# RWKV-6 attention with a mixture-of-depths block: reordering GpSimd's and ScalarE's turn, the loads, the PSUM pair and the steps table

## The chip, the cores and the metric

The kernel runs on one core of a Trainium2 chip. The metric is the device time of one execution in microseconds (us); runs of one kernel are compared by their medians.

## What is computed

The first part is a recurrence over 768 positions for 4 batches of 8 heads of 48 dimensions. The second part takes the 384 numbers of a position (8 heads side by side) as one row, scores the 768 rows of a batch, picks the 128 best of them, sends these through a small two-layer network and adds the gated outcome to them.

```python
for t in range(S):
    cur = einsum('bhd,bhe->bhde', u * k[t], v[t])
    y[t] = einsum('bhd,bhde->bhe', r[t], state + cur)
    state = w[t][..., None] * state + einsum('bhd,bhe->bhde', k[t], v[t])
...
scores = einsum('bsd,d->bs', x, w_gate)
for b in range(B):
    top_idx = argpartition(-scores[b], 128)[:128]
    xe = x[b, top_idx]
    ye = maximum(xe @ w1, 0) @ w2            # 384 -> 1024 -> 384
    g = sigmoid(scores[b, top_idx])
    out[b, top_idx] = xe + g[:, None] * ye
```

## The kernel before

The positions of a batch are cut into 6 chunks of 128, which gives 24 chunks, numbered n from 0 to 23. The recurrence is done chunk by chunk with matrix products. Within a chunk the products of the decays are taken from the start of the chunk, so that k is multiplied by a falling factor and r by a rising one; scores inside the chunk, the contribution of the state before the chunk, and the new state are then products of these.

The program order of every engine's queue is the order in which the code issues the instructions; no scheduler changes it. One pass of the loop in the last part of the kernel is called turn n here. A turn works on several chunks at once, each at another stage:

- `loads(n + 4)` (L102) issues on SP's queue the loads of w for chunk n+8, of k and r for chunk n+7 and of v for chunk n+5. In seven early turns a piece of the network's weights follows (L545).
- `from_state(n)` (L301) multiplies r of chunk n by the state on TensorE (PE); a small copy `seen` (L309) on ScalarE (ACT) follows it.
- `lnw(n + 4)` takes on ACT the logarithm lw of w (L139) and, from it, `over` (L143).
- `divided(n + 3)` (L183) makes kw on GpSimd (POOL).
- `scores(n + 1)` (L242), `fresh(n + 1)` (L258) and `from_chunk(n)` (L318) are three more sets of 32 small matmuls on PE.
- `turned(n + 2, ...)` (L226, L228) transposes K and R on PE into a pair of PSUM tiles (`psR`, tag "r") and copies them out on ACT as Kt and Rt.
- `masked`, `states` and `result` (L270, L285, L288, L332, L338) run on VectorE (DVE): the masked scores sc, the states s1 and mid, the output x of chunk n and its score. `states` ends with the product s on POOL (L290), which needs a small row `all_buf`. `result` sends x to memory on SP's queue (L342) and needs `vo`.
- `sums(n + 4)` adds lw up on PE (L159) into a PSUM tile of the pool `psM` (tag "m", one buffer); ACT makes `fall` and `rise` (L162, L165) and, on one partition, `line_buf` (L172), and SP's queue spreads this to `all_buf` (L176).
- `scaled(n + 3)` (L216) makes K and R on DVE.
- `own_products(n + 3)` (L192, L193) makes rk on POOL in two products, the first of which waits for `scaled`; `own_values(n + 1)` (L207) makes `vo` on POOL; `own_sum(n + 2)` (L200) is on DVE.

The second part of a batch runs in the turns of the next batch, in small steps. `select(b)` is a generator with these steps: spread the scores (ps_e and `every`, twice), count for each position how many are ahead of it (`ahead`, six pieces, L369), the `rank` (ps_r, L379) and the pick matrix (`pick`, L393), then the row numbers (ps_i, L400, `idx`) and the gather of the rows (`xe`, L413, an indirect transfer from POOL's queue), the transpose of these (ps_x, L421, `xeT`), and the gate. Its PSUM tiles share the one buffer "m" with `sums`. `forward(b)` has 16 steps: eight of three products with w1 (L464), with an activation `hid` (L469) after the fourth and the eighth, and eight of one product with w2 (L474), the last of which also makes `ye` (L480) and scatters it (L483). Its PSUM tile is a single buffer "f". In the profile every such product is two matmuls.

The table `plan` says which steps a turn takes: for each sixth of a batch two strings, the first run behind `from_chunk`, the second at the end of the turn; "s" is a step of `select`, "f" one of `forward`. `forward(b)` joins the queue of steps in the turn that `plan_forward` names.

After the loop, for the last batch, the kernel first decides whether all decays were in range: a sum of `guard` on DVE (L574), a matmul (L576), a comparison `wide` (L578), and a load of it into a register on all engines (L581). Then the rest of the second part follows, in an order written out as one string. A general version for decays out of range stands behind a branch and is not taken.

Of the kernel before, what the change touches and what calls it, by code (L numbers as in the profile page):

```python
# [9 lines left out]
FP32 = mybir.dt.float32  # L10
# [3 lines left out]
AF = mybir.ActivationFunctionType  # L14
# [3 lines left out]
L = 128  # L18
# [17 lines left out]
def kernel(  # L36
# [59 lines left out]
    def load(name, n):  # L96
        if not 0 <= n < N:
            return
        b, ci = chunks[n]
        x, bufs = dict(w=(w, 5), k=(k, 5), r=(r, 5), v=(v, 6))[name]  # L100
        t = lev.tile([L, H, D], FP32, tag=name, name=name, bufs=bufs)
        nc.sync.dma_start(  # L102
            out=t, in_=x[b, :, ci * L:(ci + 1) * L, :].rearrange("h t d -> t h d")
        )
        work[n][name] = t

    def loads(n):
        load("w", n + 4)
        load("k", n + 3)
        load("r", n + 3)  # L110
        load("v", n + 1)

    weights = [
        (w1[:, c], moe_w1[c * L:(c + 1) * L, :]) for c in range(NDC)
# [38 lines left out]
    def sums(n):  # L153
        if not 0 <= n < N:
            return
        t = work[n]
        lw = t.pop("lw")
        ps = psM.tile([L, 512], FP32, tag="m", name="ps_x")
        nc.tensor.matmul(ps[:, 0:C], tri, lw, start=True, stop=True)  # L159
        t["fall"] = lev.tile([L, C], FP32, tag="fall", name="fall")  # L160
        t["rise"] = lev.tile([L, C], FP32, tag="rise", name="rise")
        nc.scalar.activation(  # L162
            out=t["fall"], in_=ps[:, 0:C], func=AF.Exp, accum_out=guard[:, n, 1:2]
        )
        nc.scalar.activation(  # L165
            out=t["rise"], in_=ps[:, 0:C], func=AF.Exp, scale=-1.0,
            accum_out=guard[:, n, 0:1],
        )
        if chunks[n][1] > 0:
            line = line_bufs[n % len(line_bufs)]  # L170
            t["all"] = all_bufs[n % len(all_bufs)]
            nc.scalar.activation(  # L172
                out=line[:, :, 0:D, :].rearrange("o q d j -> o j q d"), func=AF.Exp,
                in_=ps[0:1, 0:C].rearrange("o (j q d) -> o j q d", q=2, d=D),
            )
            nc.sync.dma_start(out=t["all"], in_=line.rearrange("o q d j -> o (q d j)"))  # L176

# [171 lines left out]
    def select(b):  # L349

        every = mod.tile([L, S], FP32, name="every")
        for hf in range(2):
            ps = psM.tile([L, NHF, L], FP32, tag="m", name="ps_e")
            for q in range(NHF):
                c = hf * NHF + q
                nc.tensor.transpose(
                    ps[:, q, :], score[:, b, c:c + 1].to_broadcast([L, L]), ident
                )
            nc.scalar.copy(  # L359
                out=every[:, hf * NHF * L:(hf + 1) * NHF * L],  # L360
                in_=ps.rearrange("p q t -> p (q t)"),
            )
            yield

        ahead = mod.tile([L, NCH, S], BF16, name="ahead")
        won = mod.tile([L, NCH], FP32, name="won", bufs=2)
        for c in range(NCH):
            lo = c * L
            nc.vector.scalar_tensor_tensor(  # L369
                out=ahead[:, c, lo:S], in0=every[:, lo:S], scalar=score[:, b, c:c + 1],  # L370
                in1=behind[:, 0:S - lo], op0=ALU.is_le, op1=ALU.mult,
                accum_out=won[:, c:c + 1],
            )
            if c != NCH - 2:
                yield
        ps = psM.tile([L, NCH], FP32, tag="m", name="ps_r")
        for c in range(NCH):
            for e in range(c + 1):
                nc.tensor.matmul(  # L379
                    ps[:, c:c + 1], ahead[:, e, c * L:(c + 1) * L], ones[:, 0:1],  # L380
                    start=(e == 0), stop=(e == c),
                )
        rank = mod.tile([L, NCH], FP32, name="rank", bufs=2)
        nc.vector.tensor_sub(rank, behind_n, won)
        nc.vector.tensor_add(rank, ps, rank)

        for gi, (c0, n) in enumerate(groups):
            pick = mod.tile([L, NCH, L], BF16, name="pick")
            at = rank
            if c0 > 0:  # L390
                at = mod.tile([L, NCH], FP32, name="at")
                nc.vector.tensor_scalar_add(out=at, in0=rank, scalar1=float(-c0))
            nc.vector.tensor_tensor(  # L393
                out=pick, in0=_heads(slots, NCH), in1=at.to_broadcast([L, NCH, L]),
                op=ALU.is_equal,
            )
            yield
            ps = psM.tile([L, 2], FP32, tag="m", name="ps_i")
            for c in range(NCH):
                nc.tensor.matmul(  # L400
                    ps, pick[:, c, :], ids[:, b, c, :], start=(c == 0), stop=(c == NCH - 1)
                )
            idx = mod.tile([L, 1], UINT32, name="idx", bufs=2)
            nc.vector.tensor_scalar(
                out=idx, in0=ps[:, 0:1], scalar1=ps[:, 1:2], scalar2=float(b * S),
                op0=ALU.add, op1=ALU.max,
            )
            rows = views[b][0:b + 1].rearrange("b s c -> (b s) c")
            where = bass.IndirectOffsetOnAxis(ap=idx[0:n, 0:1], axis=0)
            xe = mod.tile([L, C], FP32, name="xe", bufs=2)  # L410
            if n < L:
                nc.vector.memset(xe, 0.0)
            nc.gpsimd.indirect_dma_start(  # L413
                out=xe[0:n], out_offset=None, in_=rows, in_offset=where,
                bounds_check=(b + 1) * S - 1, oob_is_err=False,
            )
            yield

            ps = psM.tile([L, NDC, L], FP32, tag="m", name="ps_x")
            for dc in range(NDC):  # L420
                nc.tensor.transpose(ps[:, dc, :], xe[:, dc * L:(dc + 1) * L], ident)  # L421
            xeT = mod.tile([L, NDC, L], FP32, name="xeT", bufs=2)
            nc.scalar.copy(out=xeT, in_=ps)
            yield

            own = mod.tile([L, 1], FP32, name="own", bufs=2)
            scr = lev.tile([L, C], FP32, tag="scr", name="scr")
            nc.vector.tensor_tensor_reduce(
                out=scr, in0=xe, in1=wg_bc, scale=1.0, scalar=0.0, op0=ALU.mult, op1=ALU.add,
                accum_out=own,  # L430
            )
            neg = mod.tile([L, 1], FP32, name="neg", bufs=2)
            nc.vector.scalar_tensor_tensor(
                out=neg, in0=own, scalar=-1.0, in1=own, op0=ALU.mult, op1=ALU.min
            )
            nc.scalar.activation(out=neg, in_=neg, func=AF.Exp)
            den = mod.tile([L, 1], FP32, name="den", bufs=2)
            nc.vector.tensor_scalar_add(out=den, in0=neg, scalar1=1.0)
            nc.vector.reciprocal(out=den, in_=den)
            gate = mod.tile([L, 1], FP32, name="gate", bufs=2)  # L440
            nc.vector.scalar_tensor_tensor(
                out=gate, in0=own, scalar=0.0, in1=neg, op0=ALU.is_ge, op1=ALU.max
            )
            nc.vector.tensor_mul(gate, gate, den)
            chosen.setdefault(b, []).append((n, rows, where, xe, xeT, gate))
            yield
            if len(groups) > 1:
                yield from forward(b)
# [40 lines left out]
    def run(*steps):  # L489
        for g in steps:  # L490
            yield from g

    plan = [
        ("", "fsfsss"), ("", "fssfsf"), ("", "fsf"), ("s", "fff"), ("s", "sfff"), ("", "fff")
    ]
    plan_forward = 4 * NCH // 6
    steps = dict(s=iter(()), f=iter(()))

    def mix(what):

        for x in what:
            next(steps[x], None)
# [3 lines left out]
    with tc.manual_schedule():  # L506
# [34 lines left out]
        for n in range(-4, N):  # L541
# [10 lines left out]
                if j == plan_forward:  # L552
                    steps["f"] = run(steps["f"], forward(b))
            from_state(n)
            lnw(n + 4)
            divided(n + 3)
            scores(n + 1)
            fresh(n + 1)
# [1 line left out]
            mix(what[0])  # L560
            turned(n + 2, "K")
            turned(n + 2, "R")
            masked(n + 1)
            states(n + 1)
            result(n)
            sums(n + 4)
            scaled(n + 3)
            own_products(n + 3)
            own_values(n + 1)
            own_sum(n + 2)  # L570
            mix(what[1])

        total = setup.tile([L, 1], FP32)
        nc.vector.tensor_reduce(out=total, in_=guard, axis=AX.XY, op=ALU.add)  # L574
        ps = psM.tile([L, C], FP32, tag="m", name="ps_w")
# [3 lines left out]
            out=wide, in0=ps[0:1, 0:1], scalar1=LIMIT, scalar2=0.5, op0=ALU.is_le, op1=ALU.is_lt  # L579
        )  # L580
        wide = nc.values_load(wide, min_val=0, max_val=1)  # L581

        steps["s"] = run(steps["s"], select(B - 1))
        mix("ssssfsfsfsfsfsffff" + "s")
        mix(1000 * "f" + 1000 * "s")
        for _ in forward(B - 1, "mr"):
            pass
# [72 lines left out]
```

## Time and profile before

| | us |
|---|---|
| median of 3 runs (221.84 to 223.57) | 223.22 |
| profiled execution, its own time | 223.47 |
| profiled execution, span of the profile | 221.6 |

| engine | busy us | share of the span |
|---|---|---|
| PE | 172.4 | 78% |
| DVE | 141.6 | 64% |
| POOL | 117.6 | 53% |
| ACT | 102.2 | 46% |

The x of chunk 0 starts at 27.87 us, that of chunk 6 at 64.54, of chunk 12 at 107.24, of chunk 18 at 152.55, and that of chunk 23 at 188.67. The rest is the second part of the last batch. In a row of the order of time, the first number is the start, the second the duration in us; a bracket at the end tells how long the engine had been idle and what released it. In a row of the waits, the numbers are the total in us, the times, and the longest.

### The profile page before, as it was taken

Reading aid. Unit: us, or ns where it says so; the run is one execution under the profiler, and the core shown is the slowest. Engines: PE = TensorE matmul, PEld = TensorE weight load, DVE = VectorE, ACT = ScalarE, POOL = GpSimd, SP = SyncE. Lnnn points to the kernel's source line nnn. Section 1 sums busy time; section 2 is a strip of 40 time slices with the busy share of each in tenths; the row PEclk is TensorE's granted clock in tenths of the full one; section 3 lists DMA queues with packets and bytes.
Section 4 is the critical chain, followed back from the end, with each engine's and each line's share of the span. In section 5 each row is a group of like instructions: output and inputs, shape, how many; then the busy total and the mean of one; then the engine's idle time right before and its main releaser. Section 6 shows DMA issues by size and latency. Waiting matters only on the chain.

```text
span 221.6 us, 8505 instructions
## 1 busy us (share of the span) xinstructions
PE 172.4 (78%) x3586; PEld 138.2 (62%) x3586; DVE 141.6 (64%) x329; ACT 102.2 (46%) x261; POOL 117.6 (53%) x137
## 2 busy tenths in 40 slices
PE   2697677797859766897799869978898598686990
PEld 0465466676648665796687657867876467553950
DVE  6443177777546998695769986976499834281301
ACT  4685645476852722755666426656642101110110
POOL 3750578887176669775546497745654931001101
PEclk9998899999985985999999969999999769999997
DMA  6998997878989996996899884622011022101101
GB/s 130 209 186 168 192 176 163 177 137 224 233 199 210 213 209 166 198 230 149 180 201 210 180 179 100 157 63 73 3 40 40 4 70 74 38 1 36 38 7 40
DMA packets 108542, 29.38 MB, mean 133 GB/s; under 512 B 103376, under 2 KB 107728, under 8 KB 108496
## 3 DMA queue, kind: packets, MB, share of 16 engines
q1 hardware_dynamic: 107984, 27.18, 56.5%
q0 software_dynamic: 512, 1.57, 2.1%
q8 instruction: 30, 0.49, 1.0%
q14 instruction: 16, 0.13, 0.2%
HBM read 23.20 MB, written 5.51 MB: 130 GB/s over the span
## 4 chain that ended last, share of the span: by engine, by line
PE 27%; DVE 21%; issue 13%; POOL 11%; DMA 9%; ACT 9%; SPq 8%; POOLq 0%; DVEq 0%; ACTq 0%
SPq L102 6%; DMA all_buf<-line_buf 5%; PE ps_p L318 5%; PE ps_f L464 5%; DVE ahead L369 5%; PE ps_t L226 5%; POOL rk L192 3%; DVE scr L338 3%; POOL vo L207 3%; DVE x L332 3%; PE ps_f L474 3%; POOL rk L193 2%; DVE k_buf L216 2%; DMA xe<-out_dram,idx 2%; PE ps_p L242 2%
## 5 line engine op out<-in xcount | busy, mean ns | idle before, releaser
L192 POOL TENSOR_TENSOR rk<-r,k 128x384 f32<-128x384 f32 x24 | 24.4, 1015 | 20.7 <-DVE r_buf L216 19.4
L228 ACT COPY Kt<-ps_t 128x512 f32<-128x512 f32 x24 | 14.0, 585 | 45.1 <-PE ps_t L226 45.1
L318 PE MATMUL ps_p<-v,sc 64*64 64x48 f32 x768 | 30.8, 230 | 4.4 <-issue 2.6
L290 POOL TENSOR_TENSOR s<-mid,all_buf 128x192 f32<-128x192 f32 x20 | 12.2, 610 | 38.7 <-DMA all_buf<-line_buf 24.1
L318 PEld LDWEIGHTS ps_p<-v,sc 64*64 64x64 f32 x768 | 28.0, 146 | 5.6 <-issue 3.0
L159 PE MATMUL ps_x<-lw,tri 128*128 128x384 f32 x48 | 23.9, 585 | 6.4 <-ACT lw L139 6.4
L369 DVE SCALAR_TENSOR_TENSOR ahead<-every,score,behind 128x768 bf16<-128x768 f32 (+5 forms) x24 | 23.4, 1024 | 8.2 <-ACT every L359 8.2
L464 PE MATMUL ps_f<-xeT,w 128*128 128x128 f32 x192 | 24.5, 278 | 4.5 <-ACT hid L469 3.9
L464 PEld LDWEIGHTS ps_f<-xeT,w 128*128 128x128 f32 x192 | 23.1, 192 | 7.5 <-ACT hid L469 4.5
L193 POOL TENSOR_TENSOR rk<-rk,u_bc 128x384 f32<-128x384 f32 x24 | 25.2, 1050 | 1.9
L183 POOL TENSOR_TENSOR kw<-k,over 128x384 f32<-128x384 f32 x24 | 24.4, 1018 | 3.0 <-DMA k<-in_k_dram 2.9
L474 PE MATMUL ps_f<-w,hid 128*128 128x384 f32 x64 | 25.3, 529 | 0.7 <-ACT hid L469 0.7
L270 DVE TENSOR_TENSOR sc<-ps_p,mask 128x512 f32<-128x512 f32 x24 | 16.4, 682 | 14.7 <-PE ps_p L258 14.7
L332 DVE TENSOR_TENSOR x<-ps_p,vo 128x384 f32<-128x384 f32 x24 | 13.3, 552 | 17.4 <-POOL vo L207 14.5
L207 POOL TENSOR_TENSOR vo<-v,own 128x384 f32<-128x384 f32 x24 | 23.2, 966 | 0.0
L242 PE MATMUL ps_p<-Rt,Kt 48*64 48x64 f32 x768 | 17.7, 229 | 5.6 <-DVE x L332 3.2
L301 PEld LDWEIGHTS ps_p<-s,Rt 48*64 48x64 f32 x704 | 13.5, 135 | 13.4 <-issue 7.3
L242 PEld LDWEIGHTS ps_p<-Rt,Kt 48*64 48x64 f32 x768 | 15.0, 141 | 7.3 <-ACT over L143 2.0
L226 PE MATMUL ps_t<-ident,k_buf 128*128 128x128 f32 x96 | 18.7, 327 | 0.0
L301 PE MATMUL ps_p<-s,Rt 48*64 48x48 f32 x704 | 16.4, 223 | 2.5 <-DVE mid L288 2.5
L474 PEld LDWEIGHTS ps_f<-w,hid 128*128 128x128 f32 x64 | 12.6, 208 | 8.0 <-issue 1.8
L226 PE MATMUL ps_t<-ident,r_buf 128*128 128x128 f32 x96 | 17.2, 310 | 0.0
(77 smaller groups left out, 301.8 us busy)
## 6 DMA issues: line engine op xcount, KB each, us to landing
w<-in_w_dram SPq DMA_DIRECT2D x24, 192.0 KB, 4.0
k<-in_k_dram SPq DMA_DIRECT2D x24, 192.0 KB, 4.4
r<-in_r_dram SPq DMA_DIRECT2D x24, 192.0 KB, 4.7
v<-in_v_dram SPq DMA_DIRECT2D x24, 192.0 KB, 4.0
out_dram<-x SPq DMA_DIRECT2D x24, 192.0 KB, 2.8
w<-in_moe_w_dram SPq DMA_DIRECT2D x3, 512.0 KB, 5.2
w<-in_moe_w_dram SPq DMA_DIRECT2D x4, 384.0 KB, 5.2
all_buf<-line_buf SPq DMA_DIRECT2D x20, 2.0 KB, 2.6
```

What stands on the lines that cost most here:

```text
L159: nc.tensor.matmul(ps[:, 0:C], tri, lw, start=True, stop=True)
L183: nc.gpsimd.tensor_mul(t["kw"], t["k"], t.pop("over").rearrange("p (h d) -> p h d", d=D))
L192: sync(nc.gpsimd.tensor_mul(rk, t.pop("r"), t.pop("k")), t["scaled"], "one port")
L193: nc.gpsimd.tensor_mul(rk, rk, u_bc)
L207: nc.gpsimd.tensor_mul(t["vo"], t["v"], t.pop("own").to_broadcast([L, H, D]))
L226: nc.tensor.transpose(ps[:, j, :], t[name][:, 2 * j:2 * j + 2, :], ident)
L242: nc.tensor.matmul(P[half(sub), par, j * HB:(j + 1) * HB], t["Kt"][half(par, D), j, half(sub)], t["Rt"][half(par, D), j, half(sub)], start ...
L301: nc.tensor.matmul(t["P"][half(sub), par, j * D:(j + 1) * D], t["Rt"][half(par, D), j, half(sub)], t["s1" if sub else "s0"][half(par, D), ...
L318: nc.tensor.matmul(t["P"][half(sub), par, j * D:(j + 1) * D], t["sc"][half(sub), par, j, :], t["v"][half(sub), 2 * j + par, :], start=(sub ...
L369: nc.vector.scalar_tensor_tensor(out=ahead[:, c, lo:S], in0=every[:, lo:S], scalar=score[:, b, c:c + 1], in1=behind[:, 0:S - lo], op0=ALU. ...
L464: nc.tensor.matmul(ps[:, q, :], w1[:, dc, (f0 + q) * L:(f0 + q + 1) * L], xeT[:, dc, :], start=(dc == 0), stop=(dc == NDC - 1),)
L474: nc.tensor.matmul(ps, hid[:, fc, :], w2[:, fc, :], start=(fc == 0), stop=(fc == NFC - 1))
```

## The change

Seven things are moved or redirected, and no arithmetic is changed:

- `own_values(n + 1)` goes from behind `own_products` to the first place in POOL's turn.
- `lnw(n + 4)` goes from its place behind `from_state` to behind `turned`.
- the loads are issued in the order v, k, r, w.
- the activation that makes `line_buf` goes through its elements in the order of its output instead of that of its input.
- the PSUM tiles of `select` come from the pair of the transposes.
- the steps table is new: the row numbers (`idx`) come a turn after `pick`, and `forward` begins a turn later, in the sixth turn.
- the range check is issued behind the gather of the last batch, and the order after the loop is new.

```diff
     def loads(n):
-        load("w", n + 4)
+        load("v", n + 1)
         load("k", n + 3)
         load("r", n + 3)
-        load("v", n + 1)
+        load("w", n + 4)
...
             nc.scalar.activation(
-                out=line[:, :, 0:D, :].rearrange("o q d j -> o j q d"), func=AF.Exp,
-                in_=ps[0:1, 0:C].rearrange("o (j q d) -> o j q d", q=2, d=D),
+                out=line[:, :, 0:D, :], func=AF.Exp,
+                in_=ps[0:1, 0:C].rearrange("o (j q d) -> o q d j", q=2, d=D),
             )
...
-            ps = psM.tile([L, NHF, L], FP32, tag="m", name="ps_e")
+            ps = psR.tile([L, NHF, L], FP32, tag="r", name="ps_e")
...
-        ps = psM.tile([L, NCH], FP32, tag="m", name="ps_r")
+        ps = psR.tile([L, NCH], FP32, tag="r", name="ps_r")
...
-            ps = psM.tile([L, 2], FP32, tag="m", name="ps_i")
+            ps = psR.tile([L, 2], FP32, tag="r", name="ps_i")
...
-            ps = psM.tile([L, NDC, L], FP32, tag="m", name="ps_x")
+            ps = psR.tile([L, NDC, L], FP32, tag="r", name="ps_x")
...
     plan = [
-        ("", "fsfsss"), ("", "fssfsf"), ("", "fsf"), ("s", "fff"), ("s", "sfff"), ("", "fff")
+        ("", "fssfs"), ("", "fsfsf"), ("", "fsfs"), ("", "fsff"), ("", "fsff"), ("s", "sfff")
     ]
-    plan_forward = 4 * NCH // 6
+    plan_forward = 5 * NCH // 6
...
             from_state(n)
-            lnw(n + 4)
+            own_values(n + 1)
             divided(n + 3)
...
             turned(n + 2, "K")
             turned(n + 2, "R")
+            lnw(n + 4)
             masked(n + 1)
             states(n + 1)
             result(n)
             sums(n + 4)
             scaled(n + 3)
             own_products(n + 3)
-            own_values(n + 1)
             own_sum(n + 2)
             mix(what[1])
 
+        steps["s"] = run(steps["s"], select(B - 1))
+        mix("sssfsfsfsfsfsffs")
         total = setup.tile([L, 1], FP32)
...
         wide = nc.values_load(wide, min_val=0, max_val=1)
-
-        steps["s"] = run(steps["s"], select(B - 1))
-        mix("ssssfsfsfsfsfsffff" + "s")
         mix(1000 * "f" + 1000 * "s")
```

## The prediction

> **What bounds the kernel now.** I call the loop's pass over chunk n "turn n" (n from 0 to 23, six to a batch). I read the slices of the page first, then the waits, then the order of time in single turns. A number before a row is its start in us.
>
> ```profile
> PEclk9998899999985985999999969999999769999997
> DMA  6998997878989996996899884622011022101101
> ```
>
> A slice is 5.54 us. To about 107 us the transfers are nearly always busy, afterwards they thin out. The clock falls to about half in four short places.
>
> ```profile
> ACT Kt L228 <- PE ps_t L226: 45.1, 21, 5.3
> POOL s L290 <- DMA all_buf<-line_buf: 24.1, 8, 9.5
> ...
> DVE x L332 <- POOL vo L207: 14.5, 9, 2.1
> ...
> PE ps_i L400 <- DVE pick L393: 7.2, 4, 2.4
> ...
> PE ps_e L356 <- ACT line_buf L172: 4.3, 3, 1.9
> ```
>
> GpSimd's state product s waits 24.1 us for its small row all_buf, which stands in SP's queue behind the loads. Every one of the nine waits of x for vo lies before 93 us. The two PE waits, behind pick and behind line_buf, are in every batch. ScalarE waits 45.1 us for the transposes: it is early at Kt, so what it does just before Kt is free. From turn 12 on nothing waits for transfers and PE sets the pace. Turn 12 in order of time:
>
> ```profile
> 104.41 0.49 PE L301 MATMUL ps_p<-s,Rt 48*64 48x48 f32 x10
> ...
> 105.18 0.53 ACT L139 ACTIVATE lw<-w 128x384 f32<-128x384 f32 x1
> ...
> 106.78 0.66 PE L226 MATMUL ps_t<-ident,k_buf 128*128 128x128 f32 x4
> ...
> 107.27 0.60 PE L226 MATMUL ps_t<-ident,r_buf 128*128 128x128 f32 x4
> 107.47 0.59 ACT L228 COPY Kt<-ps_t 128x512 f32<-128x512 f32 x1 [1.15 <-PE ps_t L226]
> ...
> 107.71 0.81 PE L159 MATMUL ps_x<-lw,tri 128*128 128x384 f32 x2
> ...
> 107.95 0.59 ACT L228 COPY Rt<-ps_t 128x512 f32<-128x512 f32 x1
> ...
> 108.56 0.49 ACT L162 ACTIVATE fall<-ps_x 128x384 f32<-128x384 f32 x1
> ...
> 110.38 0.54 PE L356 MATMUL ps_e<-ident,score 128*128 128x128 f32 x3 [1.20 <-ACT line_buf L172]
> ...
> 111.97 0.68 PE L301 MATMUL ps_p<-s,Rt 48*64 48x48 f32 x32
> ```
>
> The reader is to see that PE goes from the transposes (107.27) straight into the sums (107.71), because lw has been ready since 105.7. A turn of PE is 2.38 (L301 to the first transposes, 104.41 to 106.78), 0.93 (two sets of transposes), 0.65 (sums), together 3.96, and then what the steps table adds.
>
> ```profile
> 129.55 0.32 PE L400 MATMUL ps_i<-ids,pick 128*128 128x2 bf16 x6 [2.42 <-DVE pick L393]
> ...
> 129.73 1.09 PE L226 MATMUL ps_t<-ident,k_buf 128*128 128x128 f32 x4
> ...
> 131.47 1.49 PE L159 MATMUL ps_x<-lw,tri 128*128 128x384 f32 x2
> ```
>
> In turn 15 PE waits 2.42 us for pick, and then transposes and sums run at 1.09 and 1.49 instead of 0.66 and 0.81. After the loop:
>
> ```profile
> 191.54 0.19 PE L576 MATMUL ps_w<-ones_f,total 128*1 128x1 f32 x2
> ...
> 192.50 0.51 PE L356 MATMUL ps_e<-ident,score 128*128 128x128 f32 x3 [0.77 <-DVE wide L578]
> ...
> 204.09 0.52 PE L421 MATMUL ps_x<-ident,xe 128*128 128x128 f32 x3 [1.18 <-DMA xe<-out_dram,idx]
> ```
>
> From L421 to the end there are 17.5 us that no edit touches.
>
> **The edits that cost nothing on the path.** *v times own first.* GpSimd's order kw, s, rk, rk, vo becomes vo, kw, s, rk, rk. Read around the turn, that is the same row of five (1.02 + 0.61 + 1.02 + 1.05 + 0.97 = 4.67 us); kw still comes right behind a vo. Only the chunk differs: x finds its vo a turn early. This takes the 14.5 us of waits, all before turn 12, where s is held by all_buf anyway. What is late next is s: the row for chunk 13 was issued at 99.57 and its s ran at 101.98. *v before w in the loads.* The bytes are the same, and all_buf stays last, so SP's queue gives the rows at the same times; if the cover goes, x of chunk 0 could come 1.9 us earlier (s at 24.51 and its 0.51, then s1, mid and a start at 25.9 instead of 27.87), which the next row takes back. *The line activation* writes in order and reads with steps. It costs between 0.49 (fall, in order on both sides) and some 0.85 (now); the nearest row is fall, and I take 0.53, good for 0.3 us in the one turn of a batch where hid behind it holds PE.
>
> The Trainium skill ("SBUF — State Buffer", in the note on cachelines) speaks against a gain: it gives PSUM lines of 8 bytes and SBUF lines of 16, so the step moves from one slow side to another. By that note line stays at 0.85 or above; the trace has no stepped PSUM read of this length, and the sum would rise by 0.6.
>
> *Second part's PSUM tiles in the transposes' pair.* Takes PE's wait behind line_buf, 1.2 us in turn 12. The pair is free when ps_e comes, since Kt and Rt are copied by then; rank's tile and idx's tile are read a turn before the transposes need them. If not, R's transposes wait for DVE.
>
> **The edit that costs: lnw behind the transposes.** Two activations (lw 0.53, over 0.52) move from the free place ahead of Kt to behind Rt. Kt starts 0.69 after the K transposes, Rt 0.48 later, the next activation 0.61 later, lw takes 0.53, and the semaphore some 0.09: PE's sums can start 2.4 us after the K transposes instead of 0.93. PE stands 1.47 us. Queued behind it on PE are the forward matmuls, ps_e and the next turn's L301; on ScalarE, fall, rise, line, hid and every are later by the same amount. This applies in turns up to 19 (n + 4 < 24). It lies under the transfers before turn 12. Bounds: 0, if PE were not first in the turn, and 1.47.
>
> **Turns 12 to 17** (before: 104.41 to 149.71, 45.3 us). Six times 3.96 is 23.8. Sixteen forward steps: eight L464 steps at 0.72 (18 matmuls in 2.17) and eight L474 at 0.70 (2.10 for three) are 11.4. The select's matmuls: ps_e 0.95, ps_r 0.65, ps_i 0.25, ps_x 0.55, together 2.4. Bare work 37.6; before has 7.7 us of waits and slow clock on top (2.42 pick, 1.2 line_buf, 1.62 for hid in turn 17, some 1.6 of half clock, rest small). After: no pick and line_buf wait and no slow clock, but 6 x 1.47 = 8.8, 0.65 for hid (now f, s, s, f in one turn) and 0.3 for xe: 47.3. That is +2.0. DVE keeps up, since ahead is spread 1, 2, 3 instead of 2, 4.
>
> **Turns 18 to 23** (from L301 of turn 18 at 149.71 to x of chunk 23 at 188.67: 39.0). Turn 18: 3.96 + 1.47 + 0.72 + 0.95 + 0.65 + 0.72 = 8.5; 19: 3.96 + 1.47 + 2.16 = 7.6; 20: 2.38 + 0.93 + 1.40 = 4.7; 21: 3.31 + 2.10 + 0.65 + 0.15 = 6.2; 22: 2.30 + 0.25 + 2.10 = 4.7; 23 to x: 2.2. Together 33.9, that is -5.1: the pick wait of turn 21 goes, and its half clock (six L474 took 4.05 at 176.53, elsewhere 2.10).
>
> **Up to turn 12.** The row numbers move from the turn after pick's start to the end of that turn, so the gather xe is issued behind GpSimd's two rk of turn 10 and read in turn 11: half a turn instead of one. In turn 10 R ends at 95, the two rk at 97.1, then xe is issued. Landing took 3.2 to 4.8 us:
>
> ```profile
> DMA to landing us min/median/max: 3.2/3.3/4.8
> ```
>
> Batch 1 had the 4.8; I take 4.0: 101.1. PE then does ps_x 0.5, the transposes, sums after 2.4, 0.65, three L464 steps 2.16, and reaches turn 12 at 106.8 instead of 104.41: +2.4. It has stood some 6 us before, and in turn 15 a wait of 2.42 was followed by half clock; so +1.2 more. Bounds: -0.5 (issue at 95, 3.2 to land) and +4.1. I take +3.6.
>
> The skill ("TensorE: Matmul & The Clock Gate", Part 1) has the gate fall after an idle window of about 3.4 us. By that figure the 2.42 us at pick should not have been enough; the row shows that it was, so the row decides. By the rule turn 11 would pay as I have it, and half clock in turn 15 would need another cause, which would stay: +1.6 a batch.
>
> **After the loop**, counted from x of chunk 23. Forward of batch 2 began a turn later, so 13 steps are left instead of 10, and in turn 23 the first three stand ahead of ps_e. xe of batch 2 lands at 1.5, ps_x and xeT 1.1, three steps 2.2, ps_e 0.95, every 0.6, six ahead 3.65 (194.67 to 198.31), ps_r, rank and pick 1.9 with the steps between: 12.1. Then ps_i 0.3, the check with its register load 1.0 (191.54 to 192.50), six L474 steps 4.2: L421 at 17.6 instead of 15.4 (204.09 less 188.67). xe has landed at 16. +2.2. The check costs the same 1.0 us of PE, only later; its register load (some 0.5 on each engine) now stands behind the last gather on GpSimd's queue, and on SP's behind the last x, with nothing after it.
>
> **Sum** against the profiled execution (span 221.6, own time 223.47, so 1.9 around it): +3.6 + 2.0 - 5.1 + 2.2 = +2.7, span 224.3, time 226.2. The median of the runs shown, 223.22, lies 0.25 below the profiled time, which I leave. A measurement of this kernel tells about 1% from no change.
>
> **Rivals.**
> 1. *lw is hidden* (faster). If DVE or GpSimd is last in most turns, the eight waits of 1.47 in turns 12 to 19 vanish: -11.8, 214.4; if half of them, and xe in turn 11 lands early (-3), 217.3. For it: DVE is busy 36.6 of 45.3 us in batch 2, and the vo waits show it close behind. Against: in turn 13 PE ran 5.99 us without a gap. 217.3, chance 0.36.
> 2. *Gains and costs cancel*: xe in turn 11 costs nothing and the rest stays: 226.2 - 3.6 = 222.6. Chance 0.20.
> 3. *Slow clock at lw's wait* (slower still): if each wait of 1.47 brings half clock as the 2.42 did, batch 2 and turns 18 and 19 lose half a us a turn: 8 x 0.5 = 4, 230.2. It decides from a wait of about 2 us. Against: a wait of 1.62 for hid (turn 11) was followed by full speed. Chance 0.11.
> 4. *The pair does not free in time*: R's transposes wait for rank or idx, some 1 us in three turns, 229. Within the 0.11.
>
> **How the numbers follow.** The forecast has 0.33, its own range 222.5 to 229 (bounds of turn 11 and of lw's wait). Slower by over 1% is the forecast and rival 3: 0.44; within 1%: 0.20; faster: 0.36. The range reaches down to 215 for half of rival 1's spread and up to 231.
>
> **What would show it.** Right: PE's sums wait for lw some 1.4 us in each turn of batch 2; no wait for pick; x no longer waits for vo; ps_x in turn 11 waits for xe; L301 of turn 12 near 107.5. Wrong: sums start behind the transposes without a gap, or turns 12 to 17 under 44 us.

## The result, and the profile after

The changed kernel takes 235.8 us (median of 4 runs, 234.16 to 239.59); the kernel before, on the same chip, 222.53 us (220.57 to 223.57). The ratio is 1.058 with an interval of 1.046 to 1.071. Ratios here and below compare each kernel's fast runs alone, so they need not be the quotient of the medians, which take in all runs. The profiled execution took 236.65 us, its span is 234.9 us. The direction was as forecast (with a chance of 0.44 for slower, a near call); the size was not: +13.3 us of span instead of +2.7, and the time lies above the range.

The slices (5.87 us each here), then the waits (engine, line, what it waits for: us in all, times, longest) of the changed kernel:

```profile
PEclk9999999755899999965999999985999999799997
DMA  6999998979789999677734783240201113001001
```

```profile
ACT Kt L228 <- PE ps_t L226: 51.7, 22, 4.5
...
PE ps_x L159 <- ACT lw L139: 30.5, 23, 5.0
...
PE ps_x L421 <- DMA xe<-out_dram,idx: 9.1, 3, 5.7
POOL s L290 <- DMA all_buf<-line_buf: 8.7, 2, 7.7
```

PE's waits for lw grew from 6.4 us to 30.5, those for the gather xe from 1.5 to 9.1; s waits 8.7 us for its row instead of 24.1. What the trace of before had and this one lacks are the waits of x for vo, of PE for pick and of ps_e behind line_buf. Turn 12 of the changed kernel in order of time (start, us, engine, line):

```profile
115.56 0.59 ACT L228 COPY Kt<-ps_t 128x512 f32<-128x512 f32 x1 [2.19 <-PE ps_t L226]
116.04 0.59 ACT L228 COPY Rt<-ps_t 128x512 f32<-128x512 f32 x1
116.52 0.54 ACT L139 ACTIVATE lw<-w 128x384 f32<-128x384 f32 x1
117.11 0.91 PE L159 MATMUL ps_x<-lw,tri 128*128 128x384 f32 x2 [1.15 <-ACT lw L139]
...
118.52 0.82 PE L356 MATMUL ps_e<-ident,score 128*128 128x128 f32 x6
...
119.00 0.46 ACT L172 ACTIVATE line_buf<-ps_x 1x384 f32<-1x384 f32 x1
```

The sums stand behind Kt, Rt and lw and wait 1.15 us; the same wait of 1.10 to 1.15 us is in nearly every turn from turn -2 to turn 19. ps_e no longer waits, and line_buf takes 0.46 us. Turn 11:

```profile
99.50 1.21 POOL L413 DMA_INDIRECT xe<-out_dram,idx  x1 [0.17 <-DVE x L332]
...
103.70 0.88 PE L421 MATMUL ps_x<-ident,xe 128*128 128x128 f32 x3 [5.74 <-DMA xe<-out_dram,idx]
...
107.38 1.65 PE L159 MATMUL ps_x<-lw,tri 128*128 128x384 f32 x2 [1.10 <-ACT lw L139]
108.82 3.74 PE L464 MATMUL ps_f<-xeT,w 128*128 128x128 f32 x18
```

PE stands 5.74 us for the gather, and then the sums take 1.65 instead of 0.91 and the 18 matmuls L464 3.74 instead of 2.17, at half clock; turn 12 begins at 112.49.

The same in turn 17:

```profile
150.84 1.04 POOL L413 DMA_INDIRECT xe<-out_dram,idx  x1
...
155.84 0.52 PE L421 MATMUL ps_x<-ident,xe 128*128 128x128 f32 x3 [1.63 <-DMA xe<-out_dram,idx]
...
159.14 1.65 PE L159 MATMUL ps_x<-lw,tri 128*128 128x384 f32 x2 [1.10 <-ACT lw L139]
```

Here the gather is read 5.0 us after its issue, PE waits only 1.63, and the sums are again at 1.65.

The span in the stretches of the prediction, from the starts of L301, of the last x and of the last L421 (us), in the profiled execution of each kernel. The last six rows are kernels of the next section:

| kernel | up to turn 12 | turns 12 to 17 | turn 18 to x(23) | x(23) to L421 | rest | span |
|---|---|---|---|---|---|---|
| before | 104.41 | 45.30 | 38.96 | 15.42 | 17.51 | 221.6 |
| changed | 112.49 | 51.50 | 34.32 | 19.13 | 17.46 | 234.9 |
| lnw back | 106.55 | 43.15 | 30.80 | 20.60 | 17.40 | 218.5 |
| lnw and table back | 105.03 | 43.57 | 36.53 | 15.47 | 17.40 | 218.0 |
| lw a turn ahead | 106.57 | 44.47 | 33.19 | 19.33 | 17.74 | 221.3 |
| dummies at xe | 105.04 | 41.43 | 30.80 | 17.69 | 17.44 | 212.4 |
| gather a full turn | 100.64 | 41.42 | 38.28 | 15.50 | 17.76 | 213.6 |
| pair alone | 105.32 | 45.21 | 38.00 | 14.74 | 17.43 | 220.7 |

### The profile page after: what moved, and what is told of

It is laid out like the page before. It is cut to its first block, busy times and chain, and to the rows that moved or that the text cites. A ratio compares the mean times of both kernels' runs of the same rounds, so it can differ in the third digit from the quotient of the medians.

```text
span 234.9 us, 8503 instructions
## 1 busy us (share of the span) xinstructions
PE 176.3 (75%) x3586; PEld 139.9 (60%) x3586; DVE 140.5 (60%) x329; ACT 95.1 (41%) x261; POOL 117.5 (50%) x137
## 4 chain that ended last, share of the span: by engine, by line
PE 41%; DVE 16%; ACT 15%; issue 14%; DMA 8%; POOL 3%; SPq 1%; POOLq 0%; DVEq 0%
PE ps_x L159 9%; PE ps_f L464 9%; PE ps_p L318 6%; PE ps_t L226 5%; DMA xe<-out_dram,idx 5%; DVE ahead L369 4%; ACT Rt L228 3%; ACT Kt L228 3%; ACT lw L139 3%; PE ps_p L301 3%; PE ps_p L242 3%; DVE scr L338 2%; PE ps_p L258 2%; DVE x L332 2%; PE ps_f L474 2%
## 5 line engine op out<-in xcount | busy, mean ns | idle before, releaser
L159 PE MATMUL ps_x<-lw,tri 128*128 128x384 f32 x48 | 27.0, 652 | 31.6 <-ACT lw L139 30.5
L318 PE MATMUL ps_p<-v,sc 64*64 64x48 f32 x768 | 29.8, 224 | 5.1 <-issue 4.3
L369 DVE SCALAR_TENSOR_TENSOR ahead<-every,score,behind 128x768 bf16<-128x768 f32 (+5 forms) x24 | 25.9, 1121 | 12.6 <-ACT every L359 12.6
L159 PEld LDWEIGHTS ps_x<-lw,tri 128*128 128x128 f32 x48 | 8.6, 224 | 38.7 <-ACT lw L139 38.7
L464 PEld LDWEIGHTS ps_f<-xeT,w 128*128 128x128 f32 x192 | 27.6, 225 | 6.5 <-ACT hid L469 2.7
L464 PE MATMUL ps_f<-xeT,w 128*128 128x128 f32 x192 | 28.3, 310 | 3.1 <-ACT hid L469 2.0
L318 PEld LDWEIGHTS ps_p<-v,sc 64*64 64x64 f32 x768 | 26.5, 139 | 6.7 <-issue 4.9
L290 POOL TENSOR_TENSOR s<-mid,all_buf 128x192 f32<-128x192 f32 x20 | 10.8, 539 | 36.1 <-DMA all_buf<-line_buf 8.7
L474 PE MATMUL ps_f<-w,hid 128*128 128x384 f32 x64 | 23.4, 496 | 1.0 <-DVE wide L580 0.8
L216 DVE TENSOR_TENSOR k_buf<-kw,fall 128x384 f32<-128x384 f32 x24 | 14.7, 614 | 10.3 <-POOL kw L183 9.8
L301 PEld LDWEIGHTS ps_p<-s,Rt 48*64 48x64 f32 x704 | 14.2, 142 | 11.2 <-issue 4.0
L301 PE MATMUL ps_p<-s,Rt 48*64 48x48 f32 x704 | 17.2, 230 | 1.0 <-DVE mid L288 1.0
L162 ACT ACTIVATE fall<-ps_x 128x384 f32<-128x384 f32 x24 | 11.8, 491 | 14.6 <-PE ps_x L159 14.6
```

Source lines behind the costliest of these rows:

```text
L301: nc.tensor.matmul(t["P"][half(sub), par, j * D:(j + 1) * D], t["Rt"][half(par, D), j, half(sub)], t["s1" if sub else "s0"][half(par, D), ...
L318: nc.tensor.matmul(t["P"][half(sub), par, j * D:(j + 1) * D], t["sc"][half(sub), par, j, :], t["v"][half(sub), 2 * j + par, :], start=(sub ...
L369: nc.vector.scalar_tensor_tensor(out=ahead[:, c, lo:S], in0=every[:, lo:S], scalar=score[:, b, c:c + 1], in1=behind[:, 0:S - lo], op0=ALU. ...
L464: nc.tensor.matmul(ps[:, q, :], w1[:, dc, (f0 + q) * L:(f0 + q + 1) * L], xeT[:, dc, :], start=(dc == 0), stop=(dc == NDC - 1),)
L474: nc.tensor.matmul(ps, hid[:, fc, :], w2[:, fc, :], start=(fc == 0), stop=(fc == NFC - 1))
```

## The experiments

Theory A: lw, put behind the transposes on ScalarE, is read by PE's sums in the same turn, and this wait is the larger cost. Theory B: the gather xe stands half a turn ahead of its reader, and the wait with the half clock behind it is the larger cost. Theory C: the order of GpSimd or the shared PSUM pair costs.

**lnw back.**

```diff
             from_state(n)
+            lnw(n + 4)
             own_values(n + 1)
...
             turned(n + 2, "R")
-            lnw(n + 4)
```

> The changed kernel with lnw(n + 4) back ahead of the K transposes' copies (behind from_state); all else as changed. Theory A (lw behind the transposes makes PE stand, and this is the larger cost): the 23 waits of ps_x for lw (30.5 us, about 1.1 to 1.5 each in turns 12 to 19) vanish, each turn from 12 to 19 is 1.0 to 1.5 us shorter, and up to turn 12 some 2 us come back: 223 to 226 us. Theory B (the gather half a turn ahead of its reader, and the slow clock behind that wait, is the larger cost): DVE or GpSimd takes most of the place of lw, the waits for xe (5.7, 1.6 and 1.8 us) stay or grow, and the time is 230 to 234 us. Theory C (the costs come from the row order of GpSimd and the shared PSUM pair): no more than 2 us come back, 234 to 236 us.

Measured: 219.27 us (218.29 to 220.33), ratio to before 0.988 (0.981 to 0.996). Its waits:

```profile
PE ps_x L421 <- DMA xe<-out_dram,idx: 11.1, 3, 5.7
...
PE ps_x L159 <- ACT lw L139: 6.2, 4, 4.2
```

The lw waits of the loop are gone, and more than theory A asked for came back: 16.4 us of span. The rest of the change, together, is a gain of 3 us of span (2.0 by the medians, 221.3 less 219.27). The waits for xe stayed at 11.1 us, as theory B said they would; they are in this kernel too, which is still about 1% faster than before.

**Steps table back, lnw left behind the transposes.** The old plan, `plan_forward = 4 * NCH // 6` and the old order of the last steps, with the check still behind the last gather.

```diff
-        ("", "fssfs"), ("", "fsfsf"), ("", "fsfs"), ("", "fsff"), ("", "fsff"), ("s", "sfff")
+        ("", "fsfsss"), ("", "fssfsf"), ("", "fsf"), ("s", "fff"), ("s", "sfff"), ("", "fff")
...
-        mix("sssfsfsfsfsfsffs")
+        mix("ssssfsfsfsfsfs")
...
+        mix("ffff" + "s")
```

> The changed kernel with the old steps table, plan_forward and order of the last steps (the check stays behind the last gather); lnw stays behind the transposes. Theory A (lw): the lw waits of PE stay at 1.1 to 1.5 us a turn, the waits for pick come back (2.4 us a batch), so that the time is 230 to 236 us, hardly better than changed. Theory B (gather half a turn from its reader): no wait of ps_x for xe in the loop, L301 of turn 12 at about 107 instead of 112.49, turn 17 near 8 us instead of 12.47, the tail 2 to 3 us shorter, less 3 to 5 us for the pick waits and the turns 18 to 23: 226 to 230 us.

Measured: 234.47 us (232.81 to 238.05), ratio 1.054 (1.045 to 1.064), where the changed kernel has 1.058. With lnw late the new table has no net cost; theory B as the larger cause falls.

**Both back.** The two edits above together.

> lnw and the steps table both as before; what stays of the change: v times own first in GpSimd's turn, v first in the loads, the line activation in order, the second part's PSUM tiles in the transposes' pair, the check behind the last gather. Theories A and B together leave only parts without a cost on the path: the wait behind line_buf (1.2 us a batch) goes and nothing comes in its place, 218 to 222 us. Theory C (the pair or GpSimd's order costs): 225 us or more, with ps_t, ps_e or ps_r waiting for a copy or a DVE read of the pair, or s later than before by over 1 us a turn.

Measured: 218.96 us (216.73 to 220.79), ratio 0.984 (0.975 to 0.992). Theory C falls. Set beside the kernel with lnw back (0.988), the table is worth nothing either way without the lw wait too: in the table of stretches it gains 5.7 us from turn 18 to x(23) (30.80 for 36.53) and 0.4 in turns 12 to 17, and loses 1.5 up to turn 12 and 5.1 behind x(23).

**lnw moved, alone, in the kernel before.**

```diff
             from_state(n)
-            lnw(n + 4)
...
             turned(n + 2, "R")
+            lnw(n + 4)
```

> The kernel before with one edit: lnw(n + 4) moved behind the transposes. Theory A: PE waits 1.1 to 1.5 us for lw in each turn from 12 to 19 (8 to 12 us in all) and some 2 us are lost up to turn 12: 231 to 235 us. Theory B: DVE and GpSimd take up about half of these waits, 225 to 228 us. Rival (slow clock at each of these waits): turns 12 to 17 above 55 us and a time over 236 us.

Measured: median 238.25 us, the runs from 232.22 to 241.71, too far apart for a ratio; before is at 221.3. The shortest run is still 10.9 us above that. In the profiled execution, which is this shortest one, PE waits for lw as in the changed kernel:

```profile
PE ps_x L159 <- ACT lw L139: 31.4, 24, 4.4
```

Its turns 12 to 17 took 49.08 us, not over 55, so the rival (half clock at each of these waits) does not hold in this execution; why the other three took longer, 237.72 to 241.71 us, is open. Turn 11 began 5.8 us later than before (101.99 for 96.23), so most of the loss ahead of turn 12 was there by then.

**lw early, over late.** This separates what PE reads from what GpSimd reads.

```diff
             from_state(n)
+            lnw(n + 4)
...
             turned(n + 2, "R")
-            lnw(n + 4)
+            over(n + 4)
```

Here `lnw` is left with the logarithm alone, and `over` takes the second activation.

> The changed kernel with lnw split: the logarithm lw goes back ahead of the K transposes' copies, the second activation (over, which GpSimd's kw of the next turn reads) stays behind the transposes. Theory A (PE's sums wait for lw of the same turn, nothing else of the move costs): the waits of ps_x for lw go and the time is that of the kernel with lnw back, 218 to 222 us. Rival (the move costs because over comes late, so that GpSimd's kw and with it k_buf are late): 230 us or more, with waits of kw for over of about 1 us a turn.

Measured: 220.92 us (219.38 to 223.33), ratio 1.003 (0.996 to 1.011). Nearly all of the cost is gone with over still late: the sums' wait for lw is the cause, not kw. By the ratios the kernel stays 1.5% above the one with lnw back (0.988), some 3 us, which the late `over` may cost.

**lw a turn ahead, at the changed place.**

```diff
-            lnw(n + 4)
+            if n == -4:
+                lnw(0)
+            lnw(n + 5)
```

> The changed kernel with lnw at the changed place but for chunk n + 5 instead of n + 4 (and once for chunk 0 ahead of the first turn): ScalarE does the same work at the same place in its order, only the sums of the same turn do not read it. Theory A: no wait of ps_x for lw, 218 to 223 us. Rival (ScalarE's order is what costs: fall, rise and line stand 1 us later on ScalarE whatever lw is for): 228 to 235 us, with ps_x free and DVE's k_buf or s's all_buf waiting instead.

Measured: 222.46 us (220.97 to 225.09), ratio 1.002 (0.997 to 1.007). Only the first turn waits:

```profile
PE ps_x L159 <- ACT lw L139: 4.3, 1, 4.3
```

The place in ScalarE's order is nearly harmless, some 3 us above the kernel with lnw back. What costs is the reader in the same turn.

**The logarithm twice**, the same values written again, 0.53 us more in each turn.

```diff
+            nc.scalar.activation(
+                out=t["lw"], in_=t["w"].rearrange("p h d -> p (h d)"), func=AF.Ln
+            )
             nc.scalar.activation(
                 out=t["lw"], in_=t.pop("w").rearrange("p h d -> p (h d)"), func=AF.Ln
             )
```

> The changed kernel with the logarithm done twice (the same values written again), so that lw is ready 0.53 us later in every turn. Theory A in the form that the runs so far give (the way PE transposes - Kt - Rt - lw - PE sums is on the path of nearly every turn, before turn 12 as well): 20 to 24 times 0.53, so 10 to 13 us more, 245 to 249 us. The prediction's form (on the path only in turns 12 to 19, hidden under the transfers before): 8 times 0.53, 4 us more, 239 to 241 us. Rival (the cost of the move is a slow clock and not the wait): within 2 us of the changed kernel unless the mean clock falls.

Measured: median 244.98 us, the runs from 236.5 to 249.4, too far apart for a ratio. The wait grew by 11.9 us in the profiled execution (30.5 in the changed kernel):

```profile
PE ps_x L162 <- ACT lw L142: 42.4, 23, 4.8
```

Single turns show the dose best: turns 14, 15 and 16 took 7.31, 8.57 and 8.17 us against 6.76, 8.02 and 7.62 in the changed kernel, 0.55 more in each. Turn 12 began at 118.32 instead of 112.49, 5.8 later; the prediction's form, in which nothing is lost before turn 12, gives 0 there (0.5 with turn 11, where its sum does hold a wait for lw). The median, 9 us above the changed kernel, lies a little under what theory A expected. But the shortest run, 236.5 us, is within 1 us of the changed kernel's 235.8, and the profiled one took 244.15, so the whole time does not settle the rival (a slow clock and not the wait); the single turns, 0.55 longer each behind a wait that grew from 1.15 to 1.70, speak for the wait.

**Dummies at xe**, in the kernel with lnw back: matmuls that nothing reads, in the turns that wait for the gather.

```diff
+    def keep_warm(times):
+        if times:
+            ps = psM.tile([L, 512], FP32, tag="m", name="ps_w")
+            for _ in range(times):
+                nc.tensor.matmul(ps[:, 0:C], ident, wg_bc, start=True, stop=True)
...
             from_chunk(n)
+            keep_warm({11: 7, 17: 5, 23: 2}.get(n, 0))
             mix(what[0])
```

> The kernel with lnw back (219.3 us) with matmuls that nothing reads put ahead of ps_x where it waits for the gather xe: 7 in turn 11, 5 in turn 17, 2 in turn 23 (of 0.65 us each at full clock). Theory B1 (half of the cost of these waits is the half clock behind them): transposes, sums and the 18 matmuls L464 behind ps_x run at 0.6, 0.8 and 2.2 us instead of 1.06, 1.0 to 1.5 and 2.6 to 2.9, so turns 11 and 17 are 1.5 to 2.5 us shorter each: 215 to 217 us. Theory B2 (only the wait costs, the clock falls for another reason, such as a budget of work): no change or longer, 219 to 222 us.

Measured: 213.15 us (212.13 to 214.18), ratio to before 0.959 (0.949 to 0.968). That is the fastest kernel of this study, 6 us below the same kernel without the dummies. Turn 11 (line numbers are 6 higher below `keep_warm`):

```profile
97.73 2.42 PE L182 MATMUL ps_w<-wg_bc,ident 128*128 128x384 f32 x7
...
100.71 0.52 PE L427 MATMUL ps_x<-ident,xe 128*128 128x128 f32 x3 [0.56 <-DMA xe<-out_dram,idx]
101.06 0.60 PE L232 MATMUL ps_t<-ident,k_buf 128*128 128x128 f32 x4
...
102.29 0.81 PE L159 MATMUL ps_x<-lw,tri 128*128 128x384 f32 x2
...
102.94 2.17 PE L470 MATMUL ps_f<-xeT,w 128*128 128x128 f32 x18
```

and the same place without them:

```profile
101.22 0.88 PE L421 MATMUL ps_x<-ident,xe 128*128 128x128 f32 x3 [5.66 <-DMA xe<-out_dram,idx]
101.89 1.06 PE L226 MATMUL ps_t<-ident,k_buf 128*128 128x128 f32 x4
...
103.60 1.01 PE L159 MATMUL ps_x<-lw,tri 128*128 128x384 f32 x2
104.44 1.72 PE L464 MATMUL ps_f<-xeT,w 128*128 128x128 f32 x14
```

A call makes two matmuls in the profile, and the first row shows the last seven of this turn's fourteen; the last row without dummies shows 14 of its 18, which ran at full speed in both. The gather is read 0.5 us earlier with the dummies, and ps_x takes 0.52 for 0.88, a transpose set 0.60 for 1.06, the sums 0.81 for 1.01: idle time ahead of ps_x is what brought the half clock, and theory B2 falls. The gain, 6.1 us of span, is more than theory B1 expected: 1.5 up to turn 12, 1.7 in turns 12 to 17 and 2.9 behind x(23) (20.60 to 17.69), where 1.87 us of waiting had been enough to slow the matmuls L464 behind it: the first 18 took 4.21 us, with the dummies 2.27.

**The gather a full turn ahead**, in the kernel with lnw back: row numbers and gather at the end of a batch's fourth turn, their reader at the start of the sixth.

```diff
-        ("", "fssfs"), ("", "fsfsf"), ("", "fsfs"), ("", "fsff"), ("", "fsff"), ("s", "sfff")
+        ("", "fsfsss"), ("", "fssfsf"), ("", "fsf"), ("", "fsff"), ("", "fff"), ("s", "sfff")
```

> The kernel with lnw back and one more change to the steps table: every, ahead and pick in the old rhythm, the row numbers and the gather at the end of the fourth turn of a batch (a turn behind pick), the second part's transposes at the start of the sixth (more than a turn behind the gather). Theory B (the table's gain at pick was eaten by the waits for xe in turns 11, 17 and 23, 5.7 + 3.5 + 1.9 us and the half clock behind them): neither pick nor xe is waited for, 210 to 215 us, turn 17 at 7 to 8 us instead of 12. Rival (DVE's older steps in two and four ahead a turn make DVE last, as they did before): the xe waits go but turns 12 to 14 are longer, 216 to 220 us.

Measured: 215.83 us (215.12 to 218.36), ratio 0.971 (0.964 to 0.978). The waits for xe fell from 11.1 to 1.2 us and turn 17 from 11.99 to 6.74, but turn 18 took 12.43 instead of 6.94, for a reason neither theory had:

```profile
146.64 0.20 ACT L436 ACTIVATE neg<-neg 128x1 f32<-128x1 f32 x1 [5.08 <-DVE neg L433]
146.75 0.14 ACT L309 COPY seen<-ps_p 128x2 f32<-128x2 f32 x1
...
146.95 1.73 PE L318 MATMUL ps_p<-v,sc 64*64 64x48 f32 x32 [3.38 <-ACT seen L309]
```

A one-column activation of the second part stands 5.08 us at the head of ScalarE's queue, waiting for DVE; `seen` is behind it, and L318 on PE waits 3.38 us for `seen`. The wait moved from PE's queue to ScalarE's. In turn 12 PE waits 1.93 us for `seen` too, and the turn takes 9.41 us instead of 6.94. The time lies between what the two theories expected.

**Two parts alone, in the kernel before.** The pair: the tiles ps_e, ps_r, ps_i and the second part's ps_x from `psR` (tag "r"). vo first: `own_values(n + 1)` ahead of `divided(n + 3)`.

> The kernel before with one edit: the second part's PSUM tiles in the transposes' pair. The prediction's step (the wait behind line_buf goes, 1.2 us a batch, nothing new waits): 218 to 220 us. Rival 4 of the prediction (the pair is not free in time, about 1 us in three turns): 223 to 226 us.

Measured: 221.3 us (220.07 to 223.64), ratio 1.002 (0.996 to 1.008): nothing. Turn 12 is shorter by the wait behind line_buf, 6.03 us for 7.56, and turn 14 longer (7.77 for 6.72), so that turns 12 to 17 stay at 45.21. In turn 14 PE waits 1.0 us for DVE's `ahead` at ps_r and 0.4 for `mid`, not for the pair: rival 4 (the pair not free in time) falls too.

> The kernel before with one edit: own_values(n + 1) ahead of divided(n + 3) instead of behind own_products. The prediction's step (x no longer waits for vo, all of it hidden, since s waits for all_buf there anyway): 221 to 223 us. Rival 1 (the x waits, 14.5 us, are partly on the path ahead of turn 12): 217 to 220 us, L301 of turn 12 at 100 to 102 instead of 104.4. Rival 2 (s is now a vo later in each turn): 223 to 226 us.

Measured: 223.25 us (220.77 to 227.12), ratio 1.009 (1.001 to 1.016). x waits for vo no longer and nothing is won; if anything the kernel is slightly slower.

**Both back, but vo last again.** Neither part alone gains, and the kernel with lnw and table back does. Is it the two together?

```diff
-            own_values(n + 1)
             divided(n + 3)
...
             own_products(n + 3)
+            own_values(n + 1)
             own_sum(n + 2)
```

> The kernel with lnw and the steps table both back (219.0 us) with one more part undone: v times own at the end of GpSimd's turn again, as before; the pair, the line activation in order, v first in the loads and the check behind the last gather stay. Theory D (the pair takes 1.5 us from turn 12 and from turn 18, as it did alone, and only with vo a turn early is that not given back by x and DVE): 221 to 223 us, x waiting for vo again (13 to 15 us). Rival (the pair and the line activation keep their gain by themselves): 218 to 220 us.

Measured: 220.08 us (216.40 to 223.32) beside 221.56 for before, too wide for a ratio. The profiled execution has 43.55 us in turns 12 to 17, as with vo first (43.57), though x waits 11.1 us for vo again. Theory D finds no support in it. What is left between 45.2 (the pair alone) and 43.6 us lies in turns 14 to 16 (6.82, 10.07 and 6.72 us; with the pair alone 7.77, 10.30 and 7.17), and it is the order of the loads, the line activation or the place of the check; the line activation, 0.38 us shorter in each turn that makes a row, is the likeliest, but it was not tried by itself, and this stays open.

## Why the prediction was right in direction and wrong in size

The kernel with lnw back splits the result: changed less lnw back is the cost of lnw, lnw back less before is the rest.

| term of the sum | predicted: lnw | measured | predicted: the rest | measured |
|---|---|---|---|---|
| up to turn 12 | +1.5 | +5.9 | +2.1 | +2.1 |
| turns 12 to 17 | +8.8 | +8.4 | -6.8 | -2.2 |
| turn 18 to x(23) | +2.9 | +3.5 | -8.0 | -8.2 |
| x(23) to L421 | 0 | -1.5 | +2.2 | +5.2 |
| sum with the end | +13.2 | +16.4 | -10.5 | -3.1 |

(The prediction's waits for lw, 1.47 us each, are taken out of its sums: one in turn 11, where it put the sums 2.4 us behind the transposes, six in turns 12 to 17, two behind them.) Of the 10.6 us that it missed, 4.4 are lnw ahead of turn 12, 4.6 the rest in turns 12 to 17, and 1.5 the stretch behind the loop.

- **lnw in turns 12 to 19: right.** PE waited 1.15 us for lw, and turns 12, 14, 15, 16 and 18 each lost 1.4 beside lnw back, where the sum has 1.47. That the stretch comes out at 8.4 for 8.8 is partly luck: turn 13 lost 2.2 and turn 17 only 0.5.
- **lnw up to turn 12: the step that failed first.** It said that the wait "lies under the transfers before turn 12" and counted it in turn 11 alone. The transfers were busy, 88% in the changed kernel from 60 to 104 us, and the turns were still later. Beside lnw back, 2.5 us were lost when xe was read in turn 11 (103.70 for 101.22) and 3.5 more behind it, where lw's wait of 1.10 came on top of the wait for xe and the half clock lasted longer: 1.65 for the sums and 3.74 for the 18 matmuls L464, with lnw back 1.01 and 2.17. Ahead of that the loss opens in turn 4: x of chunk 4 came at 52.5 to 58.5 us in all four kernels whose sums read lw of the same turn, and at 47.3 to 50.1 in all the others. In the changed kernel the wait meets half clock there; with lnw moved alone chunk 4 came at 52.5 too while the granted clock from 35 to 50 us was 1.00, so half clock is not the whole cause, and what else there is stays open. The changed kernel in stretches of 5 us (length, then busy time of PE, PEld, DVE, ACT and POOL, the granted clock, the DMA share, GB/s), and below it the kernel with lnw back:

```profile
45.00:50.00 5.00, 3.90 (x62) 2.42 (x64) 2.32 (x5) 3.52 (x10) 3.96 (x6) 0.50 1.06 253
50.00:55.00 5.00, 4.57 (x76) 4.27 (x68) 2.35 (x6) 0.49 (x2) 0.74 (x1) 0.50 0.77 137
```

```profile
45.00:50.00 5.00, 4.90 (x160) 4.10 (x162) 4.15 (x8) 4.12 (x13) 3.96 (x5) 1.00 0.70 137
```

  Loads are issued as turns free their buffers, so a later turn pushes the transfers on instead of hiding under them; that reading fits the rows (1.06 of DMA share for 0.70 from 45 to 50 us), but it is not shown, as no run takes the transfers away.
- **xe in turn 11: right in place, time and mechanism.** With lnw back, xe was issued at 97.02 and read at 101.22, where the prediction had 97.1 and 101.1; turn 12 began 2.1 us later, which is its 3.6 without lw's 1.47. In the changed kernel the issue and the reader came 2.5 us later, since GpSimd was late too.
- **xe in turn 17: the second step that failed.** The sum allowed "0.3 for xe", and by its prices the turn is 8.4 us (3.96 + 1.47 + 0.55 + 0.3 + 2.16); it took 12.47 in the changed kernel and 11.99 with lnw back. The prediction let the gather follow GpSimd's two rk of turn 10 and forgot that order for turn 17, whose gather follows the two rk of turn 16: with lnw back the issue is at 140.14, the landing at 143.6, PE waits 3.54 us and then runs the sums in 1.49 us and the 18 matmuls L464 in 2.88, at half clock for most of it.
- **Turns 18 to 23: right**, -4.6 for -5.1. The pick wait and its half clock did go.
- **After the loop: mis-sized by clock alone.** +2.2 predicted, +3.7 in the changed kernel, +5.2 with lnw back; with the dummies it is 17.69, +2.3. The steps were counted rightly, at full clock (the terms listed up to rank and pick add up to 11.9, not 12.1, a slip of 0.2), and PE ran the first of them at half clock behind the wait for xe in turn 23.
- **The edits at nothing.** vo first: hidden, as said. The loads: x of chunk 0 came at 25.39 us for 27.87, near the 25.9 that the prediction thought possible, but with vo first alone it came at 25.37 and with the new order of the loads and vo last at 27.17, so that goes with vo's place and not with the loads'. Line activation: 0.53 predicted, 0.46 measured. The Trainium skill ("SBUF — State Buffer", the note on cachelines) as the prediction read it would have had it stay at 0.85; what the note says of steps in PSUM it says of matmuls, and the row decides: this stepped read on ScalarE cost nothing over an activation in order (0.49). The pair: the wait behind line_buf went as said, but alone it was given back in turn 14, so that the 1.2 us of turn 12 was no gain.
- **The rivals.** "lw is hidden" falls: taking the same-turn reader away brings 13 to 16 us back. "Gains and costs cancel" falls with it. "Slow clock at lw's waits" had a right half: the slow clock was there, but behind xe and in turns 4 to 6, not behind the waits of 1.15 in turns 12 to 16; and its limit of about 2 us does not hold, since 1.63 and 1.87 were followed by half clock.

## What to carry to other kernels

Before a producer is moved late in its engine's order, see whether its reader stands in the same turn: here the same move was dear with the reader in the same turn and almost free with it a turn away. Do not call a new wait in a loop hidden because another resource is busy there; ask whether that resource's own issue depends on the loop. A gather on a shared queue must be timed from the issue it gets behind that queue's work, and a wait of PE is priced with the matmuls that run at half clock behind it.

## What the runs showed of the hardware that was not expected

Waits of PE of 1.63 us (turn 17 of the changed kernel) and 1.87 us (turn 23 with lnw back) were followed by half clock, while the wait of 1.62 us for hid in turn 11 of the kernel before was not (12 matmuls L464 in 1.60 us). The half clock did not always set in with the end of the wait: behind the 3.54 us with lnw back, ps_x (0.52) and K's transposes (0.60) still ran at full speed, R's (1.02) did not. Calls of matmuls without a reader, 14 in all, put into three such waits kept what follows at full speed and took 6 us off the kernel. The Trainium skill ("TensorE: Matmul & The Clock Gate", Part 1) puts the fall at an idle window of about 3.4 us and counts it as free-running; the waits of 1.63 and 1.87 are shorter than that, and the rows decide: the length of one wait did not tell whether the clock fell. Whether a window runs free no run here shows. Gathers of 128 rows landed 3.1 to 5.5 us after their issue. The line activation on one partition took 0.84 us writing with steps to SBUF and 0.46 us reading with steps from PSUM.
